# Four other column orders for the first product of one token block

## The chip, the cores and the metric

The kernel runs on one core of a Trainium2 chip. The metric is the device time of one execution in microseconds, the median of several runs. TensorE (PE in the profile) does the matrix products, with weight loads listed apart (PEld); VectorE (DVE), ScalarE (ACT) and GpSimd (POOL) do the element-wise work; SyncE (SP) issues most of the transfers.

## The reference

An attention with decay is followed by two MLPs. The change is in the first MLP.

```python
x = attn_out.transpose(0, 2, 1, 3).reshape(1536, 512)   # attention with decay, 2 x 8 heads, 768 tokens
# first MLP: w_in 512 x 2048, w_out 2048 x 512
h = x @ w_in
g = h * np.clip(h + 3.0, 0.0, 6.0) / 6.0
x = g @ w_out
# second MLP, the same sizes
h = x @ w2_in
P = a[0] + a[1] * h + a[2] * h**2 + a[3] * h**3
Q = 1.0 + abs(b[0]) * abs(h) + abs(b[1]) * h**2
out = (P / (Q + 1e-06)) @ w2_out
```

## The kernel before

The 1536 tokens are cut into NB = 3 blocks of TB = 512. Each of the two MLPs runs over the three blocks and, within a block, over NF = 16 pieces of 128 hidden features: a step s is one block and one piece, so the first MLP is steps 0 to 47, its middle block steps 16 to 31, and the second MLP steps 48 to 95. The attention runs at the start, interleaved with the first steps; the weights are loaded and converted during the first and the third block.

Operands are kept as two fp32r tiles whose sum is the value (names ending in h and l, as wih and wil, xh and xl, gh and gl), and a product is taken as three: high by high, low by high, high by low.

A step has two parts on TensorE. `mm1(s)` is the first product: for each of the three pairings and each of KD = 4 slices of 128 input features it loads a 128x128 piece of w_in (stationary) and streams 512 token columns of xh or xl (moving) past it. All 12 matmuls add into one PSUM bank of 128 x 512 values, `hb[s % 2]`, in which a row is a hidden feature and a column a token. `mm2` is the second product of an earlier step, again 12 matmuls of 512 columns, into the four banks acc. Between them `act1` applies the nonlinearity: ScalarE and VectorE read hb as one run of 512, and a split into gh and gl by ScalarE and GpSimd follows.

The order of the instructions of each engine is written out by hand (`turns`, and a manual schedule), and engines wait for each other through semaphores: ScalarE's first operation of a step (line 278) waits for the last matmul of `mm1`, and the first matmul of a later step with the same bank waits until it was read.

Of the kernel before, what the change touches and what calls it, by code (L numbers as in the profile page):

```python
# [17 lines left out]
TB = 512  # L18
# [12 lines left out]
def fused_kernel(  # L31
# [14 lines left out]
    nc = tc.nc  # L46
# [4 lines left out]
    KD = DM // 128  # L51
    NF = DFF // 128
# [20 lines left out]
    xh = [xp.tile([128, KD, TB], F32R, name=f"xh{i}") for i in range(NB)]  # L73
    xl = [xp.tile([128, KD, TB], F32R, name=f"xl{i}") for i in range(NB)]
# [38 lines left out]
    for s in range(NSTEP):  # L113
# [5 lines left out]
        while at < to:  # L119
            d, i = quarters[at]  # L120
# [3 lines left out]
    while at < len(quarters) - 8:  # L124
        d, i = quarters[at]
# [92 lines left out]
        nc.gpsimd.tensor_tensor(lo, x, hi.bitcast(F32), op=ALU.subtract)  # L218


    def mm1(s):
        tb, f = (s // NF) % NB, s % NF
        ih, il = W["in", f]
        h = hb[s % 2]
        for kk in range(KD):
            nc.tensor.matmul(h, lhsT=ih[:, kk, :], rhs=xh[tb][:, kk, :], start=kk == 0, stop=False)  # L226
        for kk in range(KD):
            nc.tensor.matmul(h, lhsT=il[:, kk, :], rhs=xh[tb][:, kk, :], start=False, stop=False)  # L228
        for kk in range(KD):
            nc.tensor.matmul(h, lhsT=ih[:, kk, :], rhs=xl[tb][:, kk, :], start=False, stop=kk == KD - 1)  # L230

    def mm2(s, ds=(0, 1, 2, 3)):
        tb, f = (s // NF) % NB, s % NF
# [85 lines left out]
    with ExitStack() as actx:  # L319
# [129 lines left out]
        with tc.manual_schedule():  # L449
# [38 lines left out]
            for h2 in range(2):  # L488
                r = slice(64 * h2, 64 * h2 + 64)
# [44 lines left out]
            for s in range(att_steps):  # L534
                c = CPT + s
                j = s + 3
                if s == 0:
                    mm1(0)
                    conv_c(2, 0, part="clamp")
                    conv_l(2, 0, acc[2], "shift")  # L540
# [10 lines left out]
                    conv_h(2, 1)  # L551
                    load_job(j + 1)
                    mm1(1)
                    act1(1)
                    conv_all(conv_c, j)
# [5 lines left out]
                    w_tiles(wr, range(EARLY, EIN), ())  # L561
                else:
                    mm1(s + 1)
                    if s == 1:
                        att_t(c, (X, Y))
# [32 lines left out]
    with tc.manual_schedule():  # L598
# [12 lines left out]
        for at, (kind, s, *qs) in enumerate(todo):  # L611
# [3 lines left out]
            j = None  # L615
            if s + 2 < NJ1:
                j = s + 2
            elif s >= W2AT and s - W2AT + NJ1 < len(jobs):
                j = s - W2AT + NJ1
# [79 lines left out]
```

## Time and profile before

| what | value |
|---|---|
| median of 3 runs | 587.91 us (587.55 to 588.61) |
| span of the profiled execution, first to last instruction | 586.0 us |
| instructions | 8507, of them 3117 matmuls and 3117 weight loads |
| busy: TensorE / VectorE / ScalarE / GpSimd | 580.1 / 429.8 / 385.4 / 361.2 us |
| first product (lines 226, 228, 230) | 1152 matmuls of 512 columns |
| steps 16 to 31 | 141.42 to 228.46 us |

The time of the runs is longer than the span, which doesn't count what lies before the first instruction and after the last; of the profiled execution the page gives only the span, 586.0 us. A matmul's recorded duration (389 ns for 512 columns) is longer than the distance to the next one's start, since matmuls are pipelined: what one costs is read from start to start.

### The profile page before, as it was taken

Reading aid. Unit: us, or ns where it says so; the run is one execution under the profiler, and the core shown is the slowest. Engines: PE = TensorE matmul, PEld = TensorE weight load, DVE = VectorE, ACT = ScalarE, POOL = GpSimd, SP = SyncE. Lnnn points to the kernel's source line nnn. Section 1 sums busy time; section 2 is a strip of 40 time slices with the busy share of each in tenths; the row PEclk is TensorE's granted clock in tenths of the full one; section 3 lists DMA queues with packets and bytes.
Section 4 is the critical chain, followed back from the end, with each engine's and each line's share of the span. In section 5 each row is a group of like instructions: output and inputs, shape, how many; then the busy total and the mean of one; then the engine's idle time right before and its main releaser. Section 6 shows DMA issues by size and latency. Waiting matters only on the chain.

```text
span 586.0 us, 8507 instructions
## 1 busy us (share of the span) xinstructions
PE 580.1 (99%) x3117; PEld 475.4 (81%) x3117; DVE 429.8 (73%) x478; ACT 385.4 (66%) x650; POOL 361.2 (62%) x290
## 2 busy tenths in 40 slices
PE   8999999999999999999999999999999999999997
PEld 6777787888888888888888888888888888888885
DVE  6797676887211012688888999999998888999991
ACT  3686656786322223677778888888876677877771
POOL 3665757566221222476667778788776767777771
PEclk9999999999999999999999999999999999999999
DMA  9998673553000000456563001000100000100001
GB/s 184 258 263 225 160 229 126 161 162 107 1 0 1 0 1 1 165 194 182 177 196 128 2 0 37 1 1 1 73 1 0 1 1 1 72 1 0 2 1 72
DMA packets 61674, 46.69 MB, mean 80 GB/s; under 512 B 39488, under 2 KB 56128, under 8 KB 61632
## 3 DMA queue, kind: packets, MB, share of 16 engines
q1 hardware_dynamic: 61344, 46.02, 27.8%
q8 instruction: 24, 0.39, 0.3%
q10 hardware_dynamic: 288, 0.14, 0.1%
q14 instruction: 18, 0.15, 0.1%
HBM read 43.00 MB, written 3.15 MB: 79 GB/s over the span
## 4 chain that ended last, share of the span: by engine, by line
PE 96%; SPq 2%; DMA 1%; issue 0%; DVE 0%; ACT 0%
PE acc L245 45%; PE hb L226 15%; PE hb L228 15%; PE hb L230 15%; SPq L348 2%; DMA vn<-in_v_dram 1%; PE Y L391 1%; PE X L424 1%; PE Y L424 1%; PE X L413 1%; PE X L391 1%; PE hb L418 1%; PE Y L369 1%; PE X L364 1%; PE acc L391 0%; PE acc L418 0%
## 5 line engine op out<-in xcount | busy, mean ns | idle before, releaser
L314 DVE RECIPROCAL Y<-tb 128x512 f32<-128x512 f32 x48 | 161.3, 3361 | 1.6
L291 POOL TENSOR_TENSOR gl<-td,gh 128x512 fp32r<-128x512 f32 x84 | 109.1, 1298 | 82.4 <-ACT gh L290 82.4
L226 PE MATMUL hb<-xh,wih 128*128 128x512 f32 x384 | 103.8, 392 | 0.0
L228 PE MATMUL hb<-xh,wil 128*128 128x512 f32 x384 | 102.7, 389 | 0.0
L230 PE MATMUL hb<-xl,wih 128*128 128x512 f32 x384 | 102.7, 389 | 0.0
L305 POOL TENSOR_TENSOR tc<-ta,tc 128x512 f32<-128x512 f32 x48 | 62.3, 1297 | 55.0 <-ACT tc L302 55.0
L281 DVE SCALAR_TENSOR_TENSOR td<-tc,hb 128x512 f32<-128x512 f32 x48 | 32.8, 684 | 79.8 <-ACT tc L278 79.8
L230 PEld LDWEIGHTS hb<-xl,wih 128*128 128x128 f32 x384 | 72.1, 188 | 15.1
L228 PEld LDWEIGHTS hb<-xh,wil 128*128 128x128 f32 x384 | 72.1, 188 | 15.1
L226 PEld LDWEIGHTS hb<-xh,wih 128*128 128x128 f32 x384 | 71.4, 188 | 15.9 <-issue 1.4
L245 PE MATMUL acc<-gh,woh 128*128 128x512 f32 x192 | 76.1, 396 | 0.0
L245 PE MATMUL acc<-gl,woh 128*128 128x512 f32 x192 | 74.9, 390 | 0.0
L245 PE MATMUL acc<-gh,wol 128*128 128x512 f32 x192 | 74.8, 390 | 0.0
L278 ACT ACTIVATE tc<-hb,c 128x512 f32<-128x512 f32 x48 | 32.8, 684 | 60.6 <-PE hb L230 60.4
L290 ACT CAST gh<-td 128x512 fp32r<-128x512 f32 x84 | 52.0, 619 | 25.4 <-DVE td L281 13.5
L306 POOL TENSOR_TENSOR td<-td,tc 128x512 f32<-128x512 f32 x48 | 64.4, 1341 | 3.8
L218 POOL TENSOR_TENSOR wil<-ta,wih 128x512 fp32r<-128x512 f32 x32 | 41.5, 1296 | 28.2 <-ACT wih L217 28.2
L299 ACT ACTIVATE X<-hb,b_sb 128x512 f32<-128x512 f32 x48 | 31.8, 662 | 39.0 <-PE hb L230 36.2
L245 PE MATMUL acc<-woh,gh 128*128 128x512 f32 x144 | 56.0, 389 | 0.0
L245 PE MATMUL acc<-wol,gh 128*128 128x512 f32 x144 | 56.0, 389 | 0.0
L245 PE MATMUL acc<-woh,gl 128*128 128x512 f32 x144 | 56.0, 389 | 0.0
L218 POOL TENSOR_TENSOR wol<-tb,woh 128x512 fp32r<-128x512 f32 x29 | 38.4, 1326 | 14.0 <-ACT woh L217 13.4
(124 smaller groups left out, 1013.2 us busy)
## 6 DMA issues: line engine op xcount, KB each, us to landing
raw<-in_moe_w_in_dram SPq DMA_DIRECT2D x32, 512.0 KB, 4.1
raw<-in_moe_w_out_dram SPq DMA_DIRECT2D x32, 512.0 KB, 4.7
qn<-in_q_dram SPq DMA_DIRECT2D x24, 128.0 KB, 3.8
kn<-in_k_dram SPq DMA_DIRECT2D x24, 128.0 KB, 3.6
vn<-in_v_dram SPq DMA_DIRECT2D x12, 256.0 KB, 5.1
out_dram<-raw SPq DMA_DIRECT2D x11, 256.0 KB, 2.2
out_dram<-raw ACTq DMA_DIRECT2D x1, 128.0 KB, 1.8
out_dram<-raw SPq DMA_DIRECT2D x1, 128.0 KB, 1.8
```

What stands on the lines that cost most here:

```text
L218: nc.gpsimd.tensor_tensor(lo, x, hi.bitcast(F32), op=ALU.subtract)
L226: nc.tensor.matmul(h, lhsT=ih[:, kk, :], rhs=xh[tb][:, kk, :], start=kk == 0, stop=False)
L228: nc.tensor.matmul(h, lhsT=il[:, kk, :], rhs=xh[tb][:, kk, :], start=False, stop=False)
L230: nc.tensor.matmul(h, lhsT=ih[:, kk, :], rhs=xl[tb][:, kk, :], start=False, stop=kk == KD - 1)
L245: nc.tensor.matmul(acc[d], lhsT=l, rhs=r, start=st and i == 0, stop=sp and i == 2)
L278: nc.scalar.activation(t, h, AF.Relu, bias=c3)
L281: nc.vector.scalar_tensor_tensor(out=g, in0=t, scalar=6.0, in1=h, op0=ALU.min, op1=ALU.mult)
L290: nc.scalar.copy(gh, g)
L291: nc.gpsimd.tensor_tensor(gl, g, gh.bitcast(F32), op=ALU.subtract)
L305: nc.gpsimd.tensor_tensor(b1, h2, b1, op=ALU.mult)
L306: nc.gpsimd.tensor_tensor(a1, a1, b1, op=ALU.add)
L314: nc.vector.reciprocal(Y, q1)
```

## The change

In steps 16 to 31, and only there, the 12 matmuls of the first product take their moving columns in another order, and write the results in the same order, so that each token's values land where they landed before. Four steps get each of four ways: pairs of adjacent columns, alternately from the lower and the upper half of the 512 (pairs: 0, 1, 256, 257, 2, 3, ...); the same with runs of eight; from the last column to the first; and two matmuls of 256 columns each in place of one of 512, with the same stationary block. In the other steps the list of ways holds the identity alone.

```diff
+    WAYS = [
+        [lambda t: t.rearrange("p (h j e) -> p j h e", h=2, e=2)],
+        [lambda t: t.rearrange("p (h j e) -> p j h e", h=2, e=8)],
+        [lambda t: t[:, ::-1]],
+        [lambda t: t[:, 0 : TB // 2], lambda t: t[:, TB // 2 : TB]],
+    ]
+
     def mm1(s):
         tb, f = (s // NF) % NB, s % NF
         ih, il = W["in", f]
         h = hb[s % 2]
+        ways = [lambda t: t]
+        if NF <= s < 2 * NF:
+            ways = WAYS[(s - NF) // 4]
+
+        def mul(l, r, start, stop):
+            for i, way in enumerate(ways):
+                nc.tensor.matmul(way(h), lhsT=l, rhs=way(r), start=start and i == 0, stop=stop,
+                                 skip_group_check=len(ways) > 1)
+
         for kk in range(KD):
-            nc.tensor.matmul(h, lhsT=ih[:, kk, :], rhs=xh[tb][:, kk, :], start=kk == 0, stop=False)
+            mul(ih[:, kk, :], xh[tb][:, kk, :], kk == 0, False)
         for kk in range(KD):
-            nc.tensor.matmul(h, lhsT=il[:, kk, :], rhs=xh[tb][:, kk, :], start=False, stop=False)
+            mul(il[:, kk, :], xh[tb][:, kk, :], False, False)
         for kk in range(KD):
-            nc.tensor.matmul(h, lhsT=ih[:, kk, :], rhs=xl[tb][:, kk, :], start=False, stop=kk == KD - 1)
+            mul(ih[:, kk, :], xl[tb][:, kk, :], False, kk == KD - 1)
```

TensorE's order at the start of the block, before: the end of the second product of an earlier step, the first product of step 16 (hb_80 is one of the two banks, xh_85 and xl_88 the tokens of this block, wih_94 and wil_95 the weights), and the next second product.

```order
L245 MATMUL acc_79<-gl,woh_1432 128x512
L226 MATMUL hb_80<-xh_85,wih_94 128x512 x4
L228 MATMUL hb_80<-xh_85,wil_95 128x512 x4
L230 MATMUL hb_80<-xl_88,wih_94 128x512 x4
L245 MATMUL acc_76<-gh,woh_1434 128x512
```

The same place in the change, where line 238 is the one that issues the first product and line 261 the second.

```order
L261 MATMUL acc_79<-gl,woh_1432 128x512
L238 MATMUL hb_80<-xh_85,wih_94 128x128x2x2 x4
L238 MATMUL hb_80<-xh_85,wil_95 128x128x2x2 x4
L238 MATMUL hb_80<-xl_88,wih_94 128x128x2x2 x4
L261 MATMUL acc_76<-gh,woh_1434 128x512
```

Nothing has moved; the pattern has three levels (128 pairs from each of 2 halves, 2 columns at a time) in place of one. In steps 20 to 23 it reads 128x32x2x8; in steps 24 to 27 it reads 128x512 as before, with a step of -1 that this listing doesn't print.

At step 28, the first with halves, TensorE's order before is this.

```order
L245 MATMUL acc_79<-gl,woh_1424 128x512
L226 MATMUL hb_80<-xh_85,wih_1416 128x512 x4
L228 MATMUL hb_80<-xh_85,wil_1417 128x512 x4
L230 MATMUL hb_80<-xl_88,wih_1416 128x512 x4
L245 MATMUL acc_76<-gh,woh_1426 128x512
```

And in the change:

```order
L261 MATMUL acc_79<-gl,woh_1424 128x512
L238 MATMUL hb_80<-xh_85,wih_1416 128x256 x8
L238 MATMUL hb_80<-xh_85,wil_1417 128x256 x8
L238 MATMUL hb_80<-xl_88,wih_1416 128x256 x8
L261 MATMUL acc_76<-gh,woh_1426 128x512
```

Here 12 matmuls have become 24, each of which loads its stationary block (the loads are part of these rows). The other engines' instructions and their order are the same.

## Rows read from the trace of the kernel before

**Rows 1.** The page: busy time and share, granted clock by slice, chain by engine.

```profile
PE 580.1 (99%) x3117; PEld 475.4 (81%) x3117; DVE 429.8 (73%) x478; ACT 385.4 (66%) x650; POOL 361.2 (62%) x290
...
PEclk9999999999999999999999999999999999999999
...
PE 96%; SPq 2%; DMA 1%; issue 0%; DVE 0%; ACT 0%
```

**Rows 2.** Waits of TensorE: total us, times, longest us.

```profile
PE Y L477 <- DVE warm L467: 1.2, 1, 1.2
PE acc L418 <- DMA vn<-in_v_dram: 0.6, 1, 0.6
PE acc L391 <- ACT kT L370: 0.2, 1, 0.2
```

**Rows 3.** Timeline of TensorE: step 16, the starts of 17 and 32.

```profile
141.42 1.07 PE L226 MATMUL hb<-xh,wih 128*128 128x512 f32 x4
142.33 1.07 PE L228 MATMUL hb<-xh,wil 128*128 128x512 f32 x4
143.24 1.07 PE L230 MATMUL hb<-xl,wih 128*128 128x512 f32 x4
...
146.86 1.07 PE L226 MATMUL hb<-xh,wih 128*128 128x512 f32 x4
...
228.46 1.07 PE L226 MATMUL hb<-xh,wih 128*128 128x512 f32 x4
```

**Rows 4.** Windows: four steps each, then the rest to the last matmul.

```profile
core 0: us, PE busy (x) PEld busy (x) DVE busy (x) ACT busy (x) POOL busy (x), PEclk, DMA share, GB/s
141.42:163.18 21.76, 21.76 (x97) 18.02 (x96) 7.08 (x11) 8.13 (x14) 6.85 (x7) 1.00 0.00 1
163.18:184.94 21.76, 21.76 (x97) 18.02 (x96) 2.75 (x4) 5.23 (x8) 5.16 (x5) 1.00 0.00 1
184.94:206.70 21.76, 21.76 (x97) 18.02 (x96) 2.75 (x4) 5.23 (x8) 5.16 (x5) 1.00 0.00 1
206.70:228.46 21.76, 21.76 (x97) 18.02 (x96) 2.75 (x4) 5.23 (x8) 5.16 (x5) 1.00 0.00 0
228.46:582.20 353.74, 353.74 (x1561) 292.60 (x1559) 306.00 (x267) 266.78 (x435) 249.77 (x193) 1.00 0.17 53
```

**Rows 5.** Line 230 in the block: who waited for it (us, times).

```profile
L230 PE MATMUL hb<-xl,wih x64: 389/389/389, 143.2 to 225.5; 128*128 128x512 f32 x64
...
  ACT tc L278: 50.2, 16
```

**Rows 6.** Timeline of the warm-up's weight loads at the program's start.

```profile
1.65 0.15 PEld L477 LDWEIGHTS <-warm 128*128 128x128 bf16 x1 [0.28 <-issue]
2.08 0.15 PEld L477 LDWEIGHTS <-warm 128*128 128x128 bf16 x1 [0.28 <-issue]
2.51 0.15 PEld L477 LDWEIGHTS <-warm 128*128 128x128 bf16 x1 [0.28 <-issue]
```

**Rows 7.** Groups of ScalarE, by form: busy us, mean ns, then idle.

```profile
L290 ACT CAST gh<-td 128x512 fp32r<-128x512 f32 x84 | 52.0, 619 | 25.4 <-DVE td L281 13.5 <-DVE td L315 11.9
...
L165 ACT ACTIVATE ta<-raw 128x512 f32<-128x512 f32 x32 | 21.4, 668 | 1.7 <-DMA raw<-in_moe_w_in_dram 1.7
...
L177 ACT ACTIVATE X<-raw 128x512 uint32<-128x512 uint32 x22 | 13.6, 620 | 0.0
```

**Rows 8.** Timeline: transposes of 128 columns, then the first fp32r loads.

```profile
46.49 0.60 PE L364 MATMUL X<-ident,qn 128*128 128x128 f32 x4
...
46.92 0.60 PE L369 MATMUL Y<-ident,kn 128*128 128x128 f32 x4
47.25 0.19 PEld L245 LDWEIGHTS acc<-gh,woh 128*128 128x128 f32 x1
...
47.36 0.19 PEld L245 LDWEIGHTS acc<-gh,wol 128*128 128x128 f32 x1
```

**Rows 9.** Groups of weight loads, by form: busy us, mean ns, then idle.

```profile
L230 PEld LDWEIGHTS hb<-xl,wih 128*128 128x128 f32 x384 | 72.1, 188 | 15.1
```

## The prediction

> **What bounds the kernel now.** I read the page first. TensorE is busy for 99% of the span, holds 96% of the chain that ended last, and its granted clock prints as 9 tenths or more in every slice [rows 1]. Busy can still hide short waits, so the next view was what TensorE waited for: 2.0 us in the whole execution, all of it before the first MLP begins [rows 2]. The third was the timeline of the block that the change touches. Step 16 begins at 141.42 us, step 17 at 146.86, and step 32, the first of the next block, at 228.46 [rows 3]. A step has 24 matmuls of 512 columns (12 of the first product, 12 of the second), so the 384 of the block start 87.04 / 384 = 0.2267 us apart. [...]
>
> Two things follow. A nanosecond added to a matmul of this block delays everything behind it on TensorE. And nobody takes it back later: from 228.46 to the end of its last matmul at 582.20 TensorE is busy for 353.74 of 353.74 us [rows 4], so no later wait shrinks because the others got more time. Nor do the others feel it: ScalarE's first operation of a step stood idle for 3.1 us before each of the 16 steps, 50.2 us in all, waiting for the first product [rows 5]. So the change is worth the sum of what its matmuls gain or lose on TensorE, one to one.
>
> **The change part by part.** The values, the number of streamed columns (512 for each stationary block) and the engines' order stay. What changes is the order in which the moving columns are read from SBUF and, the same, the order in which their results are written (added) in the bank hb. There are 12 matmuls x 4 steps = 48 for each way. In before, every matmul of the block reads and writes one rising run of 512; no row of this trace shows TensorE with any other order, so three of the terms have to be bounded.
>
> *Pairs (steps 16 to 19).* Two adjacent columns, then a jump of 256 columns, 256 runs per matmul. Floor: no cost, as the number of columns is the same. Ceiling: the stream falls to one column where it now takes two. The nearest row for that speed is the warm-up at the start of the program, where the weight loads of its 512-column bf16 matmuls stand 0.43 us apart [rows 6]. [...] Against 0.227 us it is 0.200 us per matmul, 48 x 0.200 = +9.6 us. The nearest stepped read on another engine is ScalarE's from raw, which takes every second word: 668 and 620 ns for 512 elements, beside 619 ns for a cast that reads one run [rows 7]. So stepping through memory is nearly free at ScalarE's pace, though TensorE takes elements faster. I take 0, with the ceiling kept.
>
> *Eights (steps 20 to 23).* Runs of eight, 64 per matmul. If the pairs' ceiling were a price per jump, 0.200 us / 256 = 0.78 ns, 64 jumps would be 50 ns, or +2.4 us. I take 0; ceiling +9.6 us, if it is not the jumps but any departure from one run that costs.
>
> *Reversed (steps 24 to 27).* One run with step -1, so there are no jumps, only falling addresses. The same two ends, 0 and +9.6 us; I take 0.
>
> [...]
>
> *Halves (steps 28 to 31).* 48 matmuls of 512 columns become 96 of 256, each with a load of the same 128x128 weights: 48 matmuls and 48 loads more. The streaming itself does not grow: 2 x 256 columns. What grows is the part of the 0.2267 us that isn't streaming. [...] The load must fit behind a half: the transposes, 128 columns each with a 128x128 load, start 0.43 us apart in fours, 108 ns for one, and the first fp32r load after them makes room for the next after 0.11 us (47.25 and 47.36) [rows 8]. [...] Were the load alone the pace, two would be 218 ns and the group 0.4 us faster. If instead the recorded 188 ns of an fp32r load [rows 9] could not be shortened, two would be 376 ns, and 48 x (376 - 227) = +7.2 us. I take +0.65: the 110 ns are seen, while the 188 contain waiting, since loads of that recorded length are accepted 0.11 us apart.
>
> The waits of the other engines stay: only the last matmul of a step is waited for, in the halves the second one. The added instructions are 96 in 8507, and none stands on another engine.
>
> The sum is 0 + 0 + 0 + 0.65 us. The profiled span becomes 586.0 + 0.65, about 586.6 us. The median of the runs lies 1.9 us above the span, which is time outside the first and last instruction and stays: 587.91 + 0.65 = 588.6 us. The times shown differ among themselves by 1.06 us, 0.18%, so about 0.2%, or 1.2 us, is what a measurement here can tell from no change, and the forecast is inside that.
>
> **The rivals.**
> 1. *Pairs fall to half speed, alone.* Place: the 48 matmuls of steps 16 to 19. [...] Against it: ScalarE's cheap stepped reads. +9.6 + 0.65 gives 598.2 us, slower.
> 2. *Reversed falls to half speed, alone.* If two columns are fetched together only where the address rises by one element, a step of -1 takes them singly. The same price, 598.2 us.
> 3. *Both*: 2 x 9.6 + 0.65, 607.8 us.
> 4. *Every order that isn't one rising run costs*: 3 x 9.6 + 0.65, 617.4 us. [...]
> 5. *The halves are bound by their loads*, at 188 ns each: 587.91 + 7.2 = 595.1 us. Against it stand the 110 ns above.
> 6. *A small price per jump or per run*, some 10 to 50 ns in pairs or eights: 0.5 to 2.4 us a group, about 591 us.
> 7. *It gains*: the halves run at the load's 109 ns and the rest is free, 587.5 us. It is no more than 0.4 us and could not be told from no change.
>
> That the change does nothing is not open for the shapes: the program holds 48 matmuls more and the other access patterns on both sides. It is open for the orders, and that is the forecast.
>
> **How the numbers follow.** Forecast 0.38; pairs alone 0.17; reversed alone 0.18; both 0.10; all three 0.06; halves bound by loads 0.06; small price 0.04; gain 0.01. The free orders are the likeliest single case, yet together the cases with a price outweigh it, because three orders are tried whose price no row shows and one failure is enough. The forecast's own range is 587.5 to 589.2 us (0 to 0.65 us, with the spread of the median). The range to hold 8 in 10 runs from 587.4 to 599.0 us: it takes in the single failures, the load-bound halves and the small price, and leaves out both (0.10) and all three (0.06). Slower by over 0.2% is 0.17 + 0.18 + 0.10 + 0.06 + 0.06 + 0.04 and 0.01 from the upper edge of the forecast, 0.62; within 0.2% 0.36; faster 0.02, which is mere spread.
>
> **What would show it.** In the profile after, the four groups of the block should be 21.76, 21.76, 21.76 and about 22.4 us long, and the matmuls of the first product start 227 ns apart in the first three, 120 in the last. A group of about 31.4 us is an order at half speed and names itself: the first is pairs, the second eights, the third reversed. A last group of 29 us means that the loads bind. The forecast would be wrong in its basis if TensorE showed waits behind the block, or if the second product's matmuls, which are untouched, were no longer 227 ns apart.

## The result and the profile after

The changed kernel takes 595.68 us (median of 4 runs, 595.25 to 596.08) against 587.89 before: 7.8 us more, a ratio of 1.0131 with a 95% interval of 1.0117 to 1.0146. It is slower, inside the range of the prediction and 7.1 us over its likeliest value.

TensorE is the bound as before [rows 1]. The page's line of busy times, and what TensorE waited for:

```profile
PE 587.6 (99%) x3165; PEld 478.8 (81%) x3165; DVE 429.8 (72%) x478; ACT 385.7 (65%) x650; POOL 361.0 (61%) x290
```

```profile
PE Y L493 <- DVE warm L483: 1.3, 1, 1.3
PE acc L434 <- DMA vn<-in_v_dram: 0.7, 1, 0.7
PE acc L407 <- ACT kT L386: 0.2, 1, 0.2
```

The 48 added matmuls are there, no wait is new [rows 2], and TensorE is busy 7.5 us longer; the span is 593.5 us, 7.5 longer too. The windows of the four groups and of the rest (columns as in [rows 4]) say where:

```profile
141.53:168.81 27.28, 27.28 (x97) 18.50 (x96) 7.07 (x11) 8.16 (x14) 6.80 (x7) 1.00 0.00 1
168.81:191.40 22.59, 22.59 (x97) 18.18 (x96) 2.75 (x4) 5.23 (x8) 5.10 (x5) 1.00 0.00 1
191.40:213.56 22.16, 22.16 (x97) 18.05 (x96) 2.76 (x4) 5.22 (x8) 5.14 (x5) 1.00 0.00 1
213.56:236.04 22.48, 22.48 (x145) 20.52 (x144) 2.75 (x4) 5.24 (x8) 5.17 (x5) 1.00 0.00 1
236.04:589.78 353.74, 353.74 (x1561) 292.74 (x1559) 305.95 (x267) 266.71 (x435) 249.67 (x193) 1.00 0.17 53
```

Each group was 21.76 us [rows 4]. Pairs added 5.52, eights 0.83, reversed 0.40, halves 0.72: 7.47 us together. The rest is 353.74 us, as before to the hundredth. The other engines' busy times in the groups agree with those of before to within 0.06 us, and TensorE's granted clock prints as 1.00 throughout.

The timeline shows the pace of one way; here the first product of step 16 (pairs), 20 (eights) and 28 (halves):

```profile
142.88 1.53 PE L238 MATMUL hb<-xh,wil 128*128 128x512 f32 x4
144.24 1.53 PE L238 MATMUL hb<-xl,wih 128*128 128x512 f32 x4
...
169.78 1.14 PE L238 MATMUL hb<-xh,wil 128*128 128x512 f32 x4
170.76 1.14 PE L238 MATMUL hb<-xl,wih 128*128 128x512 f32 x4
...
214.51 1.12 PE L238 MATMUL hb<-xh,wil 128*128 128x256 f32 x8
215.47 1.12 PE L238 MATMUL hb<-xl,wih 128*128 128x256 f32 x8
```

Four matmuls take 1.36 us with pairs, 340 ns each; 0.98 with eights, about 243 each; eight halves take 0.96, 120 each. Before, four took 0.91 [rows 3]. Reversed comes to 233 in the same way. In what follows the distance from one matmul's start to the next one's is called its pace; where there is no row, it is the median over a step's first product in the trace.

### The profile page after: what moved, and what is told of

The parts are those of the page before. It is cut to its first block, busy times and chain, and to the rows that moved or that the text cites. A ratio compares the mean times of both kernels' runs of the same rounds, so it can differ in the third digit from the quotient of the medians.

```text
span 593.5 us, 8587 instructions
## 1 busy us (share of the span) xinstructions
PE 587.6 (99%) x3165; PEld 478.8 (81%) x3165; DVE 429.8 (72%) x478; ACT 385.7 (65%) x650; POOL 361.0 (61%) x290
## 4 chain that ended last, share of the span: by engine, by line
PE 96%; SPq 2%; DMA 1%; issue 0%; DVE 0%; ACT 0%
PE hb L238 46%; PE acc L261 44%; SPq L364 2%; DMA vn<-in_v_dram 1%; PE Y L407 1%; PE X L440 1%; PE Y L440 1%; PE X L429 1%; PE X L407 1%; PE hb L434 1%; PE Y L385 1%; PE X L380 1%; PE acc L407 0%; PE acc L434 0%; SPq L360 0%
## 5 line engine op out<-in xcount | busy, mean ns | idle before, releaser
L238 PE MATMUL hb<-xh,wih 128*128 128x512 f32 (+1 forms) x400 | 106.2, 390 | 0.0
L238 PE MATMUL hb<-xh,wil 128*128 128x512 f32 (+1 forms) x400 | 105.3, 387 | 0.0
L238 PE MATMUL hb<-xl,wih 128*128 128x512 f32 (+1 forms) x400 | 105.2, 387 | 0.0
L238 PEld LDWEIGHTS hb<-xh,wil 128*128 128x128 f32 x400 | 73.5, 189 | 16.4
L238 PEld LDWEIGHTS hb<-xl,wih 128*128 128x128 f32 x400 | 73.4, 189 | 16.4
L238 PEld LDWEIGHTS hb<-xh,wih 128*128 128x128 f32 x400 | 72.9, 188 | 16.5 <-issue 1.2
```

The source lines that it names most:

```text
L238: nc.tensor.matmul(way(h), lhsT=l, rhs=way(r), start=start and i == 0, stop=stop, skip_group_check=len(ways) > 1)
```

## The experiments

Since TensorE doesn't wait in this block, each step of it measures an order of its own, and one run can hold sixteen. Of the four runs that do so, each was timed and traced once; the granted clock prints as 1.00 in all their steps of this block but one (named below), and their plain steps keep 227 ns.

**Without pairs.** The first way is set back to one run.

```diff
-        [lambda t: t.rearrange("p (h j e) -> p j h e", h=2, e=2)],
+        [lambda t: t],
```

> The changed kernel with its first way, the pairs, set back to one rising run; eights, reversed and halves stay. From the starts in the trace of the changed kernel pairs added 5.52 us, eights 0.83, reversed 0.40, halves 0.72. Theory: the time is the plain sum on TensorE, so this kernel is 0.83 + 0.40 + 0.72 = 1.95 us over before, 589.8 us, a ratio of 1.0033. Rival: the four ways are not independent (a disturbed stream costs the whole block, or waits elsewhere give some back), and the time stays above 591 us or falls under 588.5.

Measured: 589.75 us against 588.08, a ratio of 1.0027 (1.0018 to 1.0036). The windows of the first two groups, each from its first matmul's start to that of the next group:

```profile
141.93:163.69 21.76, 21.76 (x97) 18.02 (x96) 7.07 (x11) 8.14 (x14) 6.85 (x7) 1.00 0.00 1
163.69:186.28 22.59, 22.59 (x97) 18.15 (x96) 2.75 (x4) 5.23 (x8) 5.12 (x5) 1.00 0.00 1
```

The first is back at 21.76 us and the others keep theirs (the third 22.16, the fourth 22.48). The medians differ by 1.67 us, and the 1.95 that the three other ways add up to lies within the interval. The ways are independent, their sum reaches the measured time, and the pairs are nearly three quarters of the loss.

**Reading or adding.** A list gives each step its pattern for the moving columns and another for the bank.

```diff
-                nc.tensor.matmul(way(h), lhsT=l, rhs=way(r), start=start and i == 0, stop=stop,
+                nc.tensor.matmul(wr(h), lhsT=l, rhs=rd(r), start=start and i == 0, stop=stop,
```

> Each of the steps 16 to 31 gets a way of its own, applied to the reading of the moving columns alone, to the adding into PSUM alone, or to both: pairs (16 to 18), quads (19 to 21), eights (22 to 24), sixteens (25 to 27), reversed (28 to 30), in that order of sides, and in step 31 single columns taken in turn from the two halves, reading alone. Where one side alone is turned, result columns land at other tokens, so that the values of this block are exchanged. Distances between matmul starts, plain 227 ns. Theory reading (memory gives the moving columns more slowly when they come from more places): pairs 340 when read, 227 when added, 340 both; eights 243, 227, 243; singles read at least 340. Theory adding (PSUM takes pairs of neighbours only in rising order without break): 227 when read, 340 when added. Theory pattern (a jump of the address costs the same cycles on whichever side it stands): 340 on each side. For reversed the same three: 233 on the side that is to blame. The price per run: if each jump costs a fixed time, quads are at 227 + 113/2 = 283, sixteens at 227 + 113/8 = 241; if lines that are read whole are free, quads are near 227 to 260.

Pace in ns:

| order | reading alone | adding alone | both |
|---|---|---|---|
| pairs | 340 | 227 | 340 |
| quads | 251 | 227 | 251 |
| eights | 243 | 227 | 243 |
| sixteens | 240 | 227 | 240 |
| reversed | 233 | 227 | 233 |
| singles, 0 256 1 257 | 216 | | |

Timeline: pairs read (142.87), pairs added (149.25), singles read (228.44), each with the row that follows it.

```profile
142.87 1.53 PE L255 MATMUL hb<-xh,wil 128*128 128x512 f32 x4
144.23 1.53 PE L255 MATMUL hb<-xl,wih 128*128 128x512 f32 x4
...
149.25 1.07 PE L255 MATMUL hb<-xh,wil 128*128 128x512 f32 x4
150.16 1.07 PE L255 MATMUL hb<-xl,wih 128*128 128x512 f32 x4
...
228.44 1.03 PE L255 MATMUL hb<-xh,wil 128*128 128x512 f32 x4
229.30 1.03 PE L255 MATMUL hb<-xl,wih 128*128 128x512 f32 x4
```

The whole price is in reading; adding is free in every order tried, 227 ns as in a plain step. A fixed price per jump fails: with half the jumps of pairs quads should pay 57 ns and pay 24, eights 28 and pay 16 (sixteens, 14, do pay 13). And the last row was foreseen by no theory: singles, with a jump at every column, are 11 ns faster than one plain run.

**Which steps of the address cost.** The same edit with other patterns.

> Each of the steps 16 to 31 gets a way of its own, in triples of reading alone, adding alone and both (result columns land at other tokens where one side alone is turned): neighbouring pairs exchanged, 2 3 0 1 6 7 4 5 (16 to 18); every other pair rising, then the others, 0 1 4 5 8 9 (19 to 21); neighbouring quads exchanged (22 to 24); the two columns of each pair exchanged, 1 0 3 2 (25 to 27); then reading alone: every second column (28), every fourth (29), every eighth (30); step 31 plain. Theory lines (what counts is how many columns are taken from a line of four fp32 values before the next line): exchanged pairs stay in a line and read at 227, every other pair reads at 340 like the pairs of the change, exchanged quads at 227 to 260, every second column at 340, every fourth and eighth at well over 340, 427 or more. Theory jumps (what counts is how often the address does not rise by one element, or an inner level of the pattern ends): exchanged pairs and every other pair 340 alike, exchanged quads 283, and every second, fourth and eighth column near 227, since their step is constant with only 2 to 8 runs. Theory distance (far jumps of 1 KB hit the same bank of memory): exchanged pairs, every other pair and quads near 227, all being near. Adding alone 227 if the price is in reading.

| order | reading alone | adding alone |
|---|---|---|
| 2 3 0 1 6 7 4 5 | 227 | 227 |
| 0 1 4 5 8 9, then the others | 452 | 227 |
| quads exchanged | 231 | 227 |
| 1 0 3 2 | 227 | 227 |
| every second column | 452 | |
| every fourth | 460 | |
| every eighth | 431 | |

Timeline: 2 3 0 1 read (142.53); 0 1 4 5 read (159.74), then added (167.03).

```profile
142.53 1.07 PE L259 MATMUL hb<-xh,wil 128*128 128x512 f32 x4
143.44 1.07 PE L259 MATMUL hb<-xl,wih 128*128 128x512 f32 x4
...
159.74 1.99 PE L259 MATMUL hb<-xh,wil 128*128 128x512 f32 x4
161.55 1.99 PE L259 MATMUL hb<-xl,wih 128*128 128x512 f32 x4
...
167.03 1.07 PE L259 MATMUL hb<-xh,wil 128*128 128x512 f32 x4
167.93 1.07 PE L259 MATMUL hb<-xl,wih 128*128 128x512 f32 x4
```

The theory of jumps falls: exchanged pairs jump as often as the pairs of the change and cost nothing, and a constant step of two costs 225 ns. Distance alone falls: 0 1 4 5 is near and at 452 the slowest of the pairs. Lines of four columns were the author's assumption, and the theory built on them holds in part: orders that stay in a group of four columns are free (227). But 340 was expected for every second column and 452 measured, about the same as for every fourth, and lines have no place for the 216 of singles.

**Pieces.**

```diff
+        16: cut(256, 256),
+        17: cut(384, 128),
...
+        23: cut(*[64] * 8),
+        24: cut(256, 256, way=PR),
```

> Steps 16 to 26 cut each matmul of the first product into pieces in rising order, each with its load of the same weights: 256+256, 384+128, 128+384, 320+192, 448+64, 192+160+160, 4x128, 8x64, and then 256+256 with pairs, eights and reversed inside each half; 27 to 31 are plain. Theory: a piece of N columns costs the larger of N/2.4 + 13.4 ns and the load's 110 ns. Sums for one former matmul: 240; 173.4 + 110 = 283; the same; 146.7 + 110 = 257; 200.1 + 110 = 310; 110 x 3 = 330; 440; 880. Pairs in halves 240 + 113 = 353, eights 257, reversed 247 (twice 6.6 if its price belongs to the matmul: 253). Rival load: the recorded 188 to 192 ns of a load bind short pieces: 4x128 at 750, 8x64 at 1500. Rival columns: the 13.4 ns belong to the columns, so halves would be 227; the changed kernel's 120 ns per half already speaks against it.

Measured per former matmul: 240, 287, 287, 257, 313, 333, 447, then 8x64, then 333 (halves of pairs), 247 (eights), 236 (reversed). The first seven are within 2% of the theory: a piece costs its columns and 13.4 ns (256 columns take 120 ns and 512 take 226.7, so 256 more cost 106.7 and some 13 are left), or some 111 ns if that is more (447 / 4 = 112 for 128 columns, 111 for 64, where the load was put at 110). Pairs inside halves cost 93 ns over plain halves, less than the 113 over a plain matmul; the price of an order is not quite a constant. The windows of the steps with halves, 4x128 and 8x64:

```profile
141.77:147.39 5.62, 5.62 (x37) 5.13 (x36) 2.58 (x4) 2.29 (x4) 2.72 (x3) 1.00 0.01 3
...
178.86:187.00 8.14, 8.14 (x62) 7.61 (x60) 0.69 (x1) 1.31 (x2) 1.34 (x2) 1.00 0.01 2
187.00:208.57 21.57, 21.57 (x110) 20.74 (x109) 0.69 (x1) 1.30 (x2) 2.20 (x2) 0.60 0.00 0
```

The 8x64 missed its 880 for a reason of its own: its pieces began 111 ns apart, as expected, but after some 3 us of them the granted clock fell (0.60 is its mean over the step) and the pieces were 213 ns apart from there on.

**Two streams.** From the orders so far a theory could be formed that has the large prices: the even and the odd places of the order are two streams, each with its own place in memory. In 0 256 1 257 one stream reads 0 1 2 3, the other 256 257 258, and each finds four columns in a group of four; in a plain run each finds two (0 2, 4 6); in 0 2 4 6 and 0 1 4 5 each finds one (0 4 8). In pairs each stream goes to and fro between two groups (0 256 2 258).

> Reading alone is turned, one order for each of the steps 16 to 28 (29 to 31 plain); result columns land at other tokens, so that the values of this block are exchanged. The runs before left this: adding costs nothing in any order; reading takes 340 ns for 0 1 256 257, 452 for 0 2 4 6 and 0 1 4 5, 227 for 2 3 0 1 and 1 0 3 2, 248 for runs of four, and 216, less than plain, for 0 256 1 257. Theory two streams: columns at even places of the order and those at odd places are fetched apart; a stream wants at least two columns of a line of four values before it goes on; four are better still (216); one that alternates between two lines stands between (340). Rival one stream: line changes of the whole order count, and 0 256 1 257 is fast for its far halves. What two streams / one stream expect: 16, 0 256 1 257 again: 216 / 216. 17, 0 8 1 9: 216 / slow. 18, 0 4 1 5 2 6 3 7: 216 / slow. 19, 0 2 1 3 4 6 5 7: 227 / 227. 20, 0 128 1 129: 216 / either. 21, 0 128 256 384 1: about 340 / slow. 22, from eight places in turn: over 340 / slow. 23, 0 256 2 258 4, then the odd columns: 227 / 452. 24, 0 256 4 260: 452 / 452. 25, the mirror of 16: 216 to 222. 26, 0 1 2 3 8 9 10 11, then the others: 227 to 240 / over 248. 27, 16 again. 28, plain, 227.

| step, order | two streams | one stream | measured |
|---|---|---|---|
| 16, 27: 0 256 1 257 | 216 | 216 | 216, 216 |
| 17: 0 8 1 9 | 216 | slow | 216 |
| 18: 0 4 1 5 2 6 3 7 | 216 | slow | 216 |
| 19: 0 2 1 3 | 227 | 227 | 227 |
| 20: 0 128 1 129 | 216 | either | 216 |
| 21: 0 128 256 384 1 | about 340 | slow | 283 |
| 22: eight places in turn | over 340 | slow | 487 |
| 23: 0 256 2 258, then the odd ones | 227 | 452 | 227 |
| 24: 0 256 4 260 | 452 | 452 | 452 |
| 25: mirror of 16 | 216 to 222 | | 216 |
| 26: 0 1 2 3 8 9 10 11 | 227 to 240 | over 248 | 231 |
| 28: plain | 227 | 227 | 227 |

Timeline of steps 18, 23, 24 and 28, second and third row of each:

```profile
153.09 1.03 PE L261 MATMUL hb<-xh,wil 128*128 128x512 f32 x4
153.96 1.03 PE L261 MATMUL hb<-xl,wih 128*128 128x512 f32 x4
...
184.03 1.07 PE L261 MATMUL hb<-xh,wil 128*128 128x512 f32 x4
184.94 1.07 PE L261 MATMUL hb<-xl,wih 128*128 128x512 f32 x4
...
190.35 1.99 PE L261 MATMUL hb<-xh,wil 128*128 128x512 f32 x4
192.17 1.99 PE L261 MATMUL hb<-xl,wih 128*128 128x512 f32 x4
...
213.82 1.07 PE L261 MATMUL hb<-xh,wil 128*128 128x512 f32 x4
214.72 1.07 PE L261 MATMUL hb<-xl,wih 128*128 128x512 f32 x4
```

Steps 23 and 24 decide: both take columns in turn from the two halves with a constant step, of two and of four, and only the number that a stream finds in a group of four differs, two or one. That is 227 against 452, where one stream expected 452 for both. So the count that goes with the price is that of each stream (one column of a group 452 ns, two 227), and not that of the whole order, in which every second column finds two of four and still takes 452. Two are not the best pace, though: four in each stream take 216, 11 ns less. Nor does the price go with how often the whole order changes its group: singles, which do so at every column, would be the slowest, and at 216 they are the fastest.

What the theory has no number for is a stream that goes to and fro between groups: 340 in pairs, 283 in step 21, 487 in step 22. Nor has it one for the small prices of orders in which each stream finds two of four: quads, eights and sixteens from the two halves (251, 243, 240) and reversed (233). There distance does count: runs of four cost 251 when taken from the two halves and 231 when taken from every second group (step 26). Why every eighth column, 431, is faster than every fourth, 460, stays open as well, and pairs were not tried at other distances.

**All matmuls turned.** The 216 ns point to a faster kernel. In before, `turn` is put on the moving operand of both products; the result's order follows from it and is undone at the output.

```diff
+    def turn(t):
+        return t.rearrange("p (h j) -> p j h", h=2)
...
-            nc.tensor.matmul(h, lhsT=ih[:, kk, :], rhs=xh[tb][:, kk, :], start=kk == 0, stop=False)
+            nc.tensor.matmul(h, lhsT=ih[:, kk, :], rhs=turn(xh[tb][:, kk, :]), start=kk == 0, stop=False)
...
-                nc.tensor.matmul(acc[d], lhsT=l, rhs=r, start=st and i == 0, stop=sp and i == 2)
+                nc.tensor.matmul(acc[d], lhsT=l, rhs=turn(r), start=st and i == 0, stop=sp and i == 2)
```

> Of before, not of the change: all 2304 matmuls of 512 columns of both MLPs read their moving operand as 0 256 1 257 2 258 and add it in rising order; the result's rows and columns are put back in place where the output is copied and stored. Theory: each start-to-start distance falls from 226.7 to 215.8 ns, as in step 31 of the run on sides, and nothing else ends last: 2304 x 10.9 ns = 25 us less, 563 us, a ratio of 0.957. It also says that the 2 to 11 ns are no fixed cost of a matmul but a matter of reading. Rivals: at 5.18 us a step VectorE (0.68 + 3.36 + 0.69 = 4.73 us a step in the second MLP, and conversions) or ScalarE end last at some steps and half of the gain is lost, 570 to 576 us; or the gain seen once in step 31 belongs to that step and is gone, 588 us.

Measured: 578.91 us against 588.03, a ratio of 0.985 (0.9834 to 0.9867), 9.1 us of the 25. The pace is 216 wherever TensorE doesn't wait, but it waits now: the page's chain has TensorE at 53% in place of 96%, VectorE at 27 and ScalarE at 10. Groups of ScalarE (columns as in [rows 7]):

```profile
L165 ACT ACTIVATE ta<-raw 128x512 f32<-128x512 f32 x32 | 26.6, 830 | 1.7 <-DMA raw<-in_moe_w_in_dram 1.7
L217 ACT CAST wih<-ta 128x512 fp32r<-128x512 f32 x32 | 19.7, 617 | 1.9 <-DVE ta L204 1.9
L177 ACT ACTIVATE X<-raw 128x512 uint32<-128x512 uint32 x22 | 18.4, 838 | 0.0
```

ScalarE's reads of every second word became slower, 830 and 838 ns instead of 668 and 620 [rows 7], while its contiguous cast took 617 (620 before). From start to start of the first product, the later steps of each stretch with conversions (12 to 15, 42 to 48) take 5.7 to 5.9 us, longer than 5.44.

**The near order, everywhere.** Two versions follow from that. One takes the order of step 18.

```diff
-        return t.rearrange("p (h j) -> p j h", h=2)
+        return t.rearrange("p (j h e) -> p j e h", h=2, e=4)
```

> As the run with every matmul turned (578.9 us, 9.1 less than before, of 25 that its 215.8 ns would give), but in the near order 0 4 1 5 2 6 3 7, in which TensorE is at two neighbouring lines instead of two that are 1 KB apart. In that run ScalarE's reads of every second word of raw took 830 and 838 ns in place of 668 and 620, while its other operations kept theirs, and the steps with conversions took some 5.9 us, longer than the 5.44 of before. Theory: the stepped reads of ScalarE and the two streams of TensorE get in each other's way in memory, whatever the distance: the same 830 ns, and 577 to 581 us. Rival: it is the far halves that collide with raw; then the reads go back to about 670 ns, the steps with conversions to 5.2 or 5.4 us, and the time to 565 to 570 us.

Measured: 574.84 us, a ratio of 0.9776 (0.976 to 0.9792). The rival was right about the place:

```profile
L165 ACT ACTIVATE ta<-raw 128x512 f32<-128x512 f32 x32 | 21.5, 671 | 2.7 <-DMA raw<-in_moe_w_in_dram 2.7
...
L177 ACT ACTIVATE X<-raw 128x512 uint32<-128x512 uint32 x22 | 13.7, 624 | 0.0
L267 ACT COPY raw<-acc 128x512 f32<-128x512 f32 x11 | 11.2, 1124 | 4.2 <-PE acc L248 4.2
```

The reads from raw are back at 671 and 624 ns. So it is TensorE's work on two far places, not its pace, that slows ScalarE's stepped reads. The gain was smaller than the rival's 565 to 570. Most steps with conversions went to 5.18 us, but the last of each stretch (14, 15 and 45 to 48) still took 5.6 to 5.7, over the rival's 5.2 or 5.4; what paces them was not taken apart. The third row, where the output copy now writes its words in the order 0 4 1 5, is another part (below).

**Turned where little is converted.** The other version is plain in the first and third block of the first MLP.

```diff
+        if s < N1 and (s // NF) % NB != 1:
+            return t
```

> Turned (0 256 1 257) only where ScalarE converts nothing or little: steps 16 to 31 and the whole second MLP, 1536 of the 2304 matmuls; plain in the first and third block of the first MLP. Theory: the loss came from the steps with conversions, so these 768 matmuls keep 226.7 ns, steps 16 to 31 give 4.2 us, and the second MLP gives between the 5 us that it gave from step 52 on in the run with all turned and 1152 x 10.9 ns = 12.6 us: 571 to 579 us. Rival: the second MLP is paced by VectorE's chain (its reciprocal of 3.36 us) as soon as TensorE needs under 5.44 us a step; then it gives nothing and the time is 583.7 us.

Measured: 576.96 us, a ratio of 0.9813 (0.98 to 0.9827). Compared with before, steps 16 to 31 gave 3.8 us, and steps 48 to 72 only 0.7; the rest of the second MLP gave 6.6. In the slow stretch most steps take 5.2 to 5.6 us, and what paces them was not taken apart. The time is inside the theory's range, and the second MLP gives some 7 of its 12.6 us, where the rival had nothing. This run also holds both orders beside each other for ScalarE's reads from raw:

```profile
L165 ACT ACTIVATE ta<-raw 128x512 f32<-128x512 f32 x32 | 21.5, 673 | 2.7 <-DMA raw<-in_moe_w_in_dram 2.7
...
L165 ACT ACTIVATE raw<-raw 128x512 f32<-128x512 f32 x3 | 2.6, 880 | 0.0
```

All but one of the first row's reads fall where TensorE is plain, the three of the second where it is turned (at 337, 359 and 380 us); in before those three took 668 ns, in the near order 671.

**The near order, with another copy.**

```diff
-                        nc.scalar.copy(turn(o), acc[d].rearrange("p (j e h) -> p j e h", h=2, e=4))
+                        nc.scalar.copy(o.rearrange("p (j h e) -> p j h e", h=2, e=4), acc[d].rearrange("p (j e h) -> p j h e", h=2, e=4))
```

> The near order everywhere, as in the run that took 574.8 us, with one edit: the 12 copies of the result read the bank in the turned order and write one rising run, where before they read one run and wrote every fourth, which took ScalarE 1124 ns in place of 593. Theory: a stepped read from PSUM is free (591 ns in the run with halves turned), so the copy takes about 593 ns; ScalarE gains 0.53 us in each of 11 copies, of which TensorE's waits for these copies, 2.4 us in all, can give back at most about 2 us: 573 to 574.8 us. Rival: ScalarE has slack there and the time stays at 574.8 within 0.2%.

Measured: 570.84 us against 587.92, a ratio of 0.971 (0.9696 to 0.9723). The copy:

```profile
L267 ACT COPY raw<-acc 128x512 f32<-128x512 f32 x11 | 5.9, 592 | 5.2 <-PE acc L248 5.2
```

The copy is at 592 ns as the theory said, but the gain is 4.0 us between the medians and 3.2 between the spans, where 2 were the bound. Of the spans' 3.2, 0.55 lie ahead of step 64, before any of these copies runs, 2.3 between there and the last matmul, and 0.4 behind it, where the last half copy takes 372 ns in place of 612. The 2.3 alone are more than the bound, because the profile's waits (2.4 us) are not all that the copies cost. Here are the first matmuls behind them, in the run before this one:

```profile
410.51 0.48 PE L248 MATMUL acc<-woh,gh 128*128 128x512 f32 x1 [2.03 <-ACT raw L267]
410.83 0.38 PE L248 MATMUL acc<-wol,gh 128*128 128x512 f32 x1
411.05 0.38 PE L248 MATMUL acc<-woh,gl 128*128 128x512 f32 x1
411.45 0.48 PE L248 MATMUL acc<-woh,gh 128*128 128x512 f32 x1
```

A wait is counted from the recorded end of the matmul ahead of it, 0.38 us after that one's start, though at the pace of 216 ns the next could have started earlier; the matmul that follows a delayed one also starts 0.32 us behind it. So 411.45 shows no wait and is still 0.40 us behind 411.05. Counted from start to start, over 216 ns each, TensorE lost 4.05 us behind these copies in that run and 1.80 in this one: 2.25, which is the 2.3. This version is 17.1 us faster than before, the best of the study.

## Why the prediction was right or wrong

**The path: right.** The block costs what TensorE loses in it, one to one: 7.47 us in the four groups, 7.5 in the span, 353.74 us behind the block unchanged, and no wait that is new. The run without pairs shows that the groups add up.

**Halves: right.** +0.65 was taken and 0.72 measured. No row of before shows how the 227 ns divide between columns and the rest, so the +0.65 was the author's estimate; what the runs show in its place is 120 ns for a half beside 226.7 for a whole, that is 106.7 ns for 256 columns and some 13 on each matmul, with the load hidden. The pieces show the same for seven cuts, with a floor of some 111 ns. The rival of loads at 188 ns is refuted.

**Pairs: wrong, and this is the step that failed.** Taken at 0, since "stepping through memory is nearly free at ScalarE's pace, though TensorE takes elements faster"; measured +5.52 us. ScalarE's rows were no bound for TensorE. The order of reading sets TensorE's pace (the run with each side alone shows it), and for pairs that pace is 340 ns; in the terms of the two streams, each goes to and fro between two groups. The rival had the place, but not the price. Not every run of two is slow: 2 3 0 1 has such runs too and costs nothing (227 ns). And the price was 5.5 us, not 9.6, a pace of 340 ns in place of 427, at which the matmuls of the warm-up follow each other in the trace of before. Nor was 427 a ceiling for orders of reading: every second column took 452, and eight places in turn 487.

**Eights and reversed: taken at 0, measured 0.83 and 0.40 us.** Both were priced as all or nothing, with the small price as a case of 0.04. Together they are about the spread of the runs. That reversed would fall to half speed, 0.18 of the chances, is refuted (233 ns); in the terms of the two streams, each finds its two columns of a group backwards as well, but the 6 ns that it costs have no explanation here.

**Adding into PSUM: free, as in the sum.** The fourth rival, a price on every order that isn't one rising run, finds nothing on the side of the bank: no order of adding that was tried changed the pace of 227 ns.

**The range held the time because one of three unpriced orders failed, at 0.6 of the price set for it.** The likeliest value, 588.6 us, was the free case, and that was wrong. That the time lies in the range says little for the mechanism: it is also within 0.6 us of the load-bound halves (595.1), which the last group refutes, so the small distance there is luck.

## What to carry to other kernels

Where TensorE streams without gaps, a wait-free stretch is a bench: each step of it can hold another variant, and the distance between starts prices it to about a nanosecond. With fp32r operands look at the moving columns in even and odd places apart, as the prices here suggest: where each took one column of a group of four before it went on, 512 columns cost 431 to 460 ns, with two of four 227 (the plain run) to 251, with all four 216. Then look again at who ends last, since of the 25 us that the pace would give 17 arrived. And price a wait from start to start where matmuls overlap: the 2.4 us of listed waits were 4.05.

## What was not expected of the hardware

- A plain run is not the fastest order for an fp32r operand: 512 columns take 227 ns in it, 216 when they are taken as 0 4 1 5 2 6 3 7. The 13 ns that a matmul pays over its columns, whole (226.7) or cut (120 for a half), are thus no fixed cost; why each matmul pays them once in a plain run stays open.
- TensorE's reading at two places 1 KB apart slowed ScalarE's reads of every second word from 620 to 838 ns; at two neighbouring places it did not (624).
- 64-column matmuls, each with a load of its own, made the granted clock fall from 1.00 to 0.50, though TensorE was never without work:

```profile
187.00:190.00 3.00, 3.00 (x29) 3.00 (x27) 0.00 (x0) 0.00 (x0) 0.92 (x1) 1.00 0.00 0
190.00:193.00 3.00, 3.00 (x17) 3.00 (x17) 0.00 (x0) 0.00 (x0) 0.00 (x0) 0.54 0.00 0
193.00:196.00 3.00, 3.00 (x16) 3.00 (x16) 0.00 (x0) 0.00 (x0) 0.00 (x0) 0.50 0.00 0
```

- A step of -1 is nearly free for the moving operand (233 ns against 227) and free for the bank (227).
